# A first attention block written out in program order on VectorE and in the transfer queue, with more of the key sums on TensorE and one weight loaded later

## The chip, the cores and the metric

The kernel runs on one core of a Trainium2 chip. The metric is the time of one execution on the device in microseconds, as the median of repeated executions. Lower is better.

## What is computed

A single-head attention of 12288 queries over 768 pooled keys is followed by two feed-forward layers. The mean over 16 positions and the product with w_sr make keys that also serve as values.

```python
def _attn_ref(q, kv, w_sr):
    kv_pool = kv.reshape(B, H // r, r, W // r, r, C).mean(axis=(2, 4))      # r = 4: 768 keys, C = 128
    k = v = kv_pool.reshape(B, -1, C) @ w_sr
    s = (q @ k.transpose(0, 2, 1)) / np.sqrt(C)
    a = np.exp(s - s.max(-1, keepdims=True))
    a /= a.sum(-1, keepdims=True) + 1e-09
    return a @ v

def _moe_ref(x, w_in, w_out, alpha):        # 128 -> 2048 -> 128
    h = x @ w_in
    return (np.maximum(h, 0.0) + alpha * np.minimum(h, 0.0)) @ w_out

def _moe2_ref(x, w_in, w_out):              # 128 -> 2048 -> 128
    h = x @ w_in
    return (h * (1.0 / (1.0 + np.exp(-1.702 * h)))) @ w_out
```

## The kernel before

**Tiles and parts.** Everything is kept transposed: 128 channels on the partitions, tokens along the free axis. There are 24 blocks (NB) of 512 tokens. Each float32 operand of the large products is scaled by a power of two and split into two float16 halves, named with h and l (qh and ql, w1h and w1l), and each product is made of three float16 matmuls (`mm3`). The four weights w1 to w4 arrive as 64-bit words, two transfers of 1 MB each (`load_w`), and are turned into halves on the chip in three steps: `stats` finds the largest value (a reduction `wm` on VectorE for each MB, a row of small operations, a matmul of ones against `diag` that spreads the maximum over the partitions, and small operations that make scales), `conv1` and `conv2` assemble the numbers (one ScalarE pass, then three VectorE operations on 128x1024), and `conv3` splits them (a ScalarE cast for the high half, a GpSimd subtraction for the low one).

**The attention of a block j** has four tiles t of 128 queries. `a_q` and `q_split` scale and split the queries. `a_s` makes the scores of a tile (six matmuls into s) and takes the negated row maximum nm on VectorE. `a_e` takes the exponential on ScalarE with the row sum sm, and the reciprocal r on VectorE. `a_h` makes the high half ah on ScalarE and issues its transposing transfer into eh. `a_l` makes the low half al on VectorE and issues the transfer into el. `a_v` multiplies with the values into xacc. `x_scale` and `x_split` turn xacc into xh and xl, which the first layer reads.

**The layers** advance in steps t, sixteen steps (KF) for a block: `l1` with its ScalarE and VectorE activation at step t, `l2` four steps later, `l3` 31 and `l4` 36 steps later (`L2_LAG`, `L3_LAG`, `L4_LAG`). So TensorE has only two layers and the attention of a coming block to do until step 31.

**The time ahead of step 0.** The input transfers are issued first: q of block 0, w1, then kv in twelve transfers (`thirds`, four for each third of the keys), then w2, q of block 1 and w3. In the first third TensorE sums the 16 positions itself, by 16 matmuls that accumulate; in the other two VectorE reduces eight 128x1024 tiles, and one matmul for each third follows. `k_max` finds the largest key of each third, `v_scale` makes the scale and splits the keys into k_hi and k_lo, `x_bound` makes a bound from alpha that the scale of x needs. Block 0's attention then runs as part of the step loop, from step -18 on, by the tables `ATT_START`, `ATT_S` and `ATT_V`. The tables `STATS` and `PREP` place the other weights in the steps; w4 is loaded after step -8 (`W4_LOAD`).

**What sets the order.** A scheduler of the framework orders each engine's instructions when the program is built, by its own estimate; the order in the Python code is where it starts from. So the order in the built program isn't that of the code, and it is fixed: on the chip each engine runs its own list, and an instruction that waits holds up all that stand behind it. The transfers are all issued from the queue of SyncE, in a list of its own.

Of the kernel before, what the change touches and what calls it, by code (L numbers as in the profile page):

```python
# [39 lines left out]
ATT_START = [-18, -5] + [KF * j - 25 for j in range(2, NB)]  # L40
ATT_S = [(0, 2, 2, 6), (0, 3, 6, 9)] + [(0, 4, 7, 12)] * (NB - 2)
ATT_V = [(5, 8, 9, 12), tuple(range(12, 18))] + [(17, 18, 19, 21, 22, 22)] * (NB - 2)
# [11 lines left out]
def attn_moe_kernel(ctx: ExitStack, tc: tile.TileContext, q, kv, w_sr, w_in1, w_out1, alpha, w_in2, w_out2, out):  # L54
# [88 lines left out]

    def stats(*keys):

        n = len(keys)
        m = small("wm", F32, 2 * NCW)
        for i, key in enumerate(keys):
            for c in range(NCW):
                nc.vector.tensor_reduce(out=m[:, i * NCW + c:i * NCW + c + 1], in_=raw[key, c][:, :, 1].bitcast(F32),  # L150
                                        axis=AX.X, op=ALU.max, apply_absolute_value=True)
# [298 lines left out]
    def thirds(i):  # L450
        tk = slice(i * TK, (i + 1) * TK)
        for n in range(4):
# [3 lines left out]
            if i == 0:  # L456
# [5 lines left out]
        if i != 0:  # L462
# [12 lines left out]
    thirds(1)  # L475
    conv2(0)
    conv3(0)
    k_max(0)
    conv2(1)
    conv3(1)  # L480
    thirds(2)
# [57 lines left out]
    def step(t):  # L539
        pieces = [(j, t - ATT_START[j]) for j in range(NB) if -8 < t - ATT_START[j] < 26]  # L540
# [23 lines left out]
        for j, p in pieces:  # L564
# [6 lines left out]
            if p == -6 and j > 0:  # L571
                a_q(j)
            if p == -4 and j > 0:
# [4 lines left out]
        for f, lag in ((x_scale, -2), (x_split, -1), (y_scale, L2_LAG + KF), (y_split, L2_LAG + KF + 2)):  # L578
            if (x := at(t, lag)) and x[1] == 0:
                f(x[0])  # L580
        if x := at(t, L3_LAG):
# [4 lines left out]

    v_scale()
    q_scale(0)
    x_bound()
    for t in range(ATT_START[0], nstep + L4_LAG):  # L590
# [4 lines left out]
        if t == W4_LOAD:  # L595
            for c in range(NCW):
                load_w("w4", c)
        if t == KV_FREE:
            kv_ctx.close()
            g_p = ctx.enter_context(tc.tile_pool(name="gp", bufs=3, reuse_waits="tile"))  # L600
# [44 lines left out]
```

## Time and profile before

| | us |
|---|---|
| median of 3 runs | 1294.38 (1294.02 to 1294.47) |
| profiled execution, its own time | 1294.28 |
| span of its instructions | 1292.5 |
| TensorE busy | 1228.2 |
| ScalarE busy | 1107.2 |
| VectorE busy | 1036.0 |
| GpSimd busy | 780.6 |

The span is what lies between the first and the last instruction; 1.8 us of the execution's time lie around it. All times in the text are microseconds from the span's start. PE is TensorE, DVE is VectorE, ACT is ScalarE, POOL is GpSimd and SPq is the transfer queue of SyncE. Lines (L347) are those of the kernel before. A busy share is an average over stages with different limits, so the stages are looked at apart.

### The profile page before, as it was taken

To read this page: it belongs to the slowest core of one execution; us is meant where nothing else is said; L and a number is where in the kernel's file an instruction comes from. 1 tells how busy PE (TensorE), PEld (TensorE's weight loads), DVE (VectorE), ACT (ScalarE), POOL (GpSimd) and SP (SyncE) were. 2 spreads that over 40 slices of the span, in tenths; PEclk is the share of its full clock that TensorE was granted. 3 is DMA by queue.
4 is the path that set the end of the run, shared out by engine and by line. 5 is a ranking of instruction groups with operands and counts; after the bars stand their busy time and mean duration, and the time that the engine had idled before them with its cause. 6 is when DMAs were issued, how large, how long until landed. Compare 5 with 4: busy or idle time off the path is not lost.

```text
span 1292.5 us, 18032 instructions
## 1 busy us (share of the span) xinstructions
PE 1228.2 (95%) x5784; PEld 567.1 (44%) x5784; DVE 1036.0 (80%) x1879; ACT 1107.2 (86%) x1964; POOL 780.6 (60%) x670
## 2 busy tenths in 40 slices
PE   3468999999999999999999999999999999999998
PEld 2323444444444444444444444444444444444443
DVE  7988899778788787887887787787888878877666
ACT  1477899899898898898898998998988988988998
POOL 1046535576675676666665665756756666667774
PEclk8678999999999999999999999999999999999999
DMA  9713312122121221211221121221212212110000
GB/s 374 169 43 56 62 33 54 37 41 54 25 54 42 37 54 33 45 42 37 48 48 38 42 54 30 49 47 32 53 33 46 49 32 43 34 37 21 9 9 17
DMA packets 165375, 66.65 MB, mean 52 GB/s; under 512 B 156448, under 2 KB 156576, under 8 KB 164256
## 3 DMA queue, kind: packets, MB, share of 16 engines
q1 hardware_dynamic: 165280, 65.51, 21.9%
q8 instruction: 45, 0.74, 0.2%
q14 instruction: 50, 0.41, 0.1%
HBM read 21.05 MB, written 6.29 MB: 21 GB/s over the span
## 4 chain that ended last, share of the span: by engine, by line
PE 55%; ACT 16%; DVE 13%; issue 5%; DMA 0%; POOLq 0%; ACTq 0%
PE h L103 8%; PE h L105 7%; PE h L104 7%; PE y L104 7%; PE y L105 7%; PE y L103 7%; DVE g L347 4%; ACT g L346 4%; ACT g L401 3%; ACT s L255 3%; DVE g L402 2%; ACT g1h L354 2%; PE xacc L103 2%; PE xacc L104 2%; PE xacc L105 2%
## 5 line engine op out<-in xcount | busy, mean ns | idle before, releaser
L355 POOL TENSOR_TENSOR g1l<-g,g1h 128x512 f16<-128x512 f32 x384 | 457.0, 1196 | 324.9 <-ACT g1h L354 308.8
L411 POOL TENSOR_TENSOR g2l<-g,g2h 128x512 f16<-128x512 f32 x272 | 315.4, 1160 | 120.5 <-ACT g2h L409 110.9
L401 ACT ACTIVATE g<-h,yu 128x512 f32<-128x512 f32 x384 | 269.4, 702 | 103.9 <-PE h L105 100.8
L402 DVE SCALAR_TENSOR_TENSOR g<-g,h 128x512 f32<-128x512 f32 x384 | 262.5, 684 | 110.6 <-ACT g L401 104.9
L347 DVE SCALAR_TENSOR_TENSOR g<-g,oma,h 128x512 f32<-128x512 f32 x384 | 284.9, 742 | 53.1 <-ACT g L346 47.1
L354 ACT CAST g1h<-g 128x512 f16<-128x512 f32 x384 | 244.3, 637 | 7.2 <-PE y L105 5.6
L346 ACT ACTIVATE g<-h 128x512 f32<-128x512 f32 x384 | 236.2, 615 | 15.3 <-PE h L105 8.0
L409 ACT CAST g2h<-g 128x512 f16<-128x512 f32 x384 | 243.8, 635 | 3.3 <-PE y L105 1.2
L104 PE MATMUL y<-g1l,w2h 128*128 128x512 f16 x384 | 145.5, 379 | 8.7 <-POOL g1l L355 8.7
L103 PE MATMUL h<-xh,w1h 128*128 128x512 f16 x384 | 146.5, 383 | 5.2 <-ACT xh L320 4.1
L103 PE MATMUL h<-yh,w3h 128*128 128x512 f16 x384 | 145.2, 378 | 4.2 <-DVE g L347 1.1
L104 PE MATMUL h<-xl,w1h 128*128 128x512 f16 x384 | 146.6, 382 | 1.4
L105 PE MATMUL h<-xh,w1l 128*128 128x512 f16 x384 | 146.7, 382 | 0.0
L103 PE MATMUL y<-g1h,w2h 128*128 128x512 f16 x384 | 145.6, 379 | 1.2 <-ACT g1h L354 1.2
L104 PE MATMUL y<-g2l,w4h 128*128 128x512 f16 x384 | 145.5, 379 | 0.5 <-POOL g2l L411 0.5
L105 PE MATMUL y<-g2h,w4l 128*128 128x512 f16 x384 | 145.5, 379 | 0.0
L105 PE MATMUL y<-g1h,w2l 128*128 128x512 f16 x384 | 145.5, 379 | 0.0
L103 PE MATMUL y<-g2h,w4h 128*128 128x512 f16 x384 | 145.5, 379 | 0.0
L105 PE MATMUL h<-yh,w3l 128*128 128x512 f16 x384 | 145.4, 379 | 0.0
L104 PE MATMUL h<-yl,w3h 128*128 128x512 f16 x384 | 145.3, 378 | 0.0
L245 DVE TENSOR_REDUCE nm<-s 128x1 f32<-128x768 f32 x96 | 91.5, 953 | 14.2 <-PE s L240 10.6
L411 DVE TENSOR_TENSOR g2l<-g,g2h 128x512 f16<-128x512 f32 x112 | 90.0, 804 | 9.7 <-ACT g2h L409 9.7
(227 smaller groups left out, 1664.8 us busy)
## 6 DMA issues: line engine op xcount, KB each, us to landing
q<-in_q SPq DMA_DIRECT2D x24, 256.0 KB, 2.6
kv<-in_kv SPq DMA_DIRECT2D x12, 512.0 KB, 9.9
out<-ob SPq DMA_DIRECT2D x24, 256.0 KB, 2.0
raw_w<-in_moe_w_in SPq DMA_DIRECT2D x4, 1024.0 KB, 9.7
raw_w<-in_moe_w_out SPq DMA_DIRECT2D x4, 1024.0 KB, 6.9
eh<-ah SPq DMA_TRANSPOSE x96, 2.7
wsr<-in_w_sr SPq DMA_DIRECT2D x1, 64.0 KB, 2.7
al<-in_moe_alpha SPq DMA_DIRECT2D x1, 8.0 KB, 1.8
```

The lines of the kernel that those rows point to most:

```text
L103: mm(out=o, lhsT=wh, rhs=xh, start=start, stop=False)
L104: mm(out=o, lhsT=wh, rhs=xl, start=False, stop=False)
L105: mm(out=o, lhsT=wl, rhs=xh, start=False, stop=stop)
L245: nc.vector.tensor_reduce(out=nm, in_=s[:, :, 0:HALF], axis=AX.XY, op=ALU.max, negate=True)
L346: nc.scalar.activation(g, h, AF.Relu, scale=-1.0)
L347: nc.vector.scalar_tensor_tensor(out=g, in0=g, scalar=oma[:, m:m + 1], in1=h, op0=ALU.mult, op1=ALU.add)
L354: nc.scalar.copy(hi, g)
L355: nc.gpsimd.tensor_tensor(out=lo, in0=g, in1=hi, op=ALU.subtract)
L401: nc.scalar.activation(g, h, AF.Tanh, scale=ysc[j][:, 0:1])
L402: nc.vector.scalar_tensor_tensor(out=g, in0=g, scalar=1.0, in1=h, op0=ALU.add, op1=ALU.mult)
L409: nc.scalar.copy(hi, g)
L411: e.tensor_tensor(out=lo, in0=g, in1=hi, op=ALU.subtract)
```

## The change

Block 0's attention leaves the step loop. Its calls are written out in the code ahead of the loop, and from `v_scale` to the end of step 2 the framework's manual schedule keeps VectorE and the transfer queue in the order of the code. ScalarE, TensorE and GpSimd are still ordered by the scheduler. TensorE sums the second third of kv too (the host lays that third out like the first), so VectorE reduces four tiles, not eight. `x_bound` stays behind `v_scale`. The query split of block 1 stands inside block 0's attention. The reductions of w2's maximum stand between pieces of the attention, w2's conversion behind it, and w4 is loaded after block 0's last transposing transfer. The reductions for w3 and w4 come at step 1, as before in the code, but VectorE may no longer do them earlier.

```diff
-ATT_START = [-18, -5] + [KF * j - 25 for j in range(2, NB)]
-KV_FREE = -11
-W4_LOAD = -8
-STATS = {-9: ("w2",), 1: ("w3", "w4")}
-PREP = [(-8, -7, -6), (-7, -6, -5), (2, 3, 4), (5, 6, 7), (10, 11, 12), (13, 14, 15)]
+ATT_START = [None, -5] + [KF * j - 25 for j in range(2, NB)]
+MANUAL_END = 2
+X_SCALE = -2
+STATS = {1: ("w3", "w4")}
+PREP = [(2, 3, 4), (5, 6, 7), (10, 11, 12), (13, 14, 15)]
...
+    def w_max(key, c, keys):
+        if keys not in wm:
+            wm[keys] = sm_p.tile([P, 2 * NCW], F32, tag="wm", name="wm")
+        i = keys.index(key) * NCW + c
+        nc.vector.tensor_reduce(out=wm[keys][:, i:i + 1], in_=raw[key, c][:, :, 1].bitcast(F32), axis=AX.X, op=ALU.max,
+                                apply_absolute_value=True)
...
-        c, p = scale_of(qsc[j], ps_x.tile([P, TB], F32, tag="x", name="qt"), None, "q")
+        c, p = scale_of(qsc[j], bank("qt"), None, "q")
...
-            if i == 0:
+            if i < 2:
                 for r in range(4):
                     mm(out=pks[i], lhsT=wsr, rhs=t[:, r * TK:(r + 1) * TK], start=n + r == 0, stop=n + r == 6)
...
-    thirds(1)
     conv2(0)
     conv3(0)
-    k_max(0)
     conv2(1)
     conv3(1)
+    k_max(0)
+    thirds(1)
     thirds(2)
...
+    manual.enter_context(tc.manual_schedule(engines={nc.vector.engine, nc.sync.engine}))
     v_scale()
     q_scale(0)
     x_bound()
-    for t in range(ATT_START[0], nstep + L4_LAG):
+    a_s(0, 0); a_s(0, 1); flush()
+    a_q(1)
+    a_e(0, 0); a_e(0, 1); flush()
+    w_max("w2", 0, ("w2",))
+    a_h(0, 0); a_l(0, 0); a_s(0, 2); flush()
+    a_h(0, 1); a_l(0, 1); a_s(0, 3); flush()
+    q_split(1); flush()
+    a_e(0, 2); a_e(0, 3); flush()
+    a_v(0, 0); a_h(0, 2); a_l(0, 2)
+    a_v(0, 1); a_h(0, 3); a_l(0, 3); flush()
...
+    q_scale(1)
+    load_q(2)
+    for c in range(NCW):
+        load_w("w4", c)
+    w_max("w2", 1, ("w2",)); stats("w2")
+    conv1(2); conv1(3)
+    a_v(0, 2); a_v(0, 3); flush()
+    conv2(2); conv3(2)
+    x_scale(0); flush()
+    x_split(0); flush()
+    conv2(3); conv3(3)
+    for t in range(ATT_START[1] - 1, nstep + L4_LAG):
...
+        if t == MANUAL_END:
+            manual.close()
```

(Calls of one piece are put on one line here.)

The built programs differ in this way at the places that matter below. The first is VectorE's list where the scores of block 0 begin: nm is the row maximum, wm the reduction of a weight, and ov to kxc are the chain of `x_bound` that starts from a matmul (pm). Before:

```order
L150 TENSOR_REDUCE wm_460<-raw_w21_247 128x1
L245 TENSOR_REDUCE nm_300<-s_293 128x1
L245 TENSOR_REDUCE nm_321<-s_314 128x1
L109 TENSOR_SCALAR nm_300<-nm_300,qu_278 128x1
L109 TENSOR_SCALAR nm_321<-nm_321,qu_278 128x1
L153 TENSOR_REDUCE wa_463<-wm_460 128x1
L150 TENSOR_REDUCE wm_615<-raw_w30_251 128x1
```

And after:

```order
L125 TENSOR_REDUCE ov_299<-pm_297 128x1
L113 TENSOR_SCALAR ab_301<-ov_299,b_w1_160 128x1
L111 TENSOR_SCALAR ab_301<-ab_301 128x1
L113 TENSOR_SCALAR kx_105<-ab_301 128x1
L113 TENSOR_SCALAR kxc_107<-kx_105 128x1
L257 TENSOR_REDUCE nm_313<-s_306 128x1
L111 TENSOR_SCALAR nm_313<-nm_313,qu_291 128x1
L257 TENSOR_REDUCE nm_321<-s_314 128x1
L111 TENSOR_SCALAR nm_321<-nm_321,qu_291 128x1
```

The weights' reductions have left the place between the scores, and the chain of `x_bound`, which the scheduler had worked into the scaling of the keys, now stands ahead of the first row maximum. The second place is VectorE's list behind the first layer's first activations, after the change: g1 is that activation for a step, nm and al are of block 1, and raw_w30 to raw_w41 are the two MB each of w3 and w4.

```order
L292 SCALAR_TENSOR_TENSOR al__608<-e_583,r_586,ah_598 128x768
L316 TENSOR_REDUCE ta_620<-q2_455 128x1
L111 TENSOR_SCALAR qd_619<-ta_620 128x1
L359 SCALAR_TENSOR_TENSOR g1_623<-g1_623,oma_104,h1_604 128x512
L257 TENSOR_REDUCE nm_618<-s_611 128x1
L111 TENSOR_SCALAR nm_618<-nm_618,qu_453 128x1
L153 TENSOR_REDUCE wm_628<-raw_w30_262 128x1
L153 TENSOR_REDUCE wm_628<-raw_w31_264 128x1
L153 TENSOR_REDUCE wm_628<-raw_w40_457 128x1
L153 TENSOR_REDUCE wm_628<-raw_w41_459 128x1
L257 TENSOR_REDUCE nm_741<-s_734 128x1
L165 TENSOR_REDUCE wa_633<-wm_628 128x2
```

All four reductions stand together behind two activations; before, they stood at four places of block 0's attention and of w2's conversion, ahead of the first layer. The third place is TensorE's list between the first layer's steps: h1 is a step's product, pm the matmul of w3's and w4's statistics that the row wa above leads to, and s the scores. The weight loads between the matmuls are left out. Before, the first two steps and what follows:

```order
L103 MATMUL h1_581<-xh_572,w1h_111 128x512
...
L103 MATMUL h1_591<-xh_572,w1h_111 128x512
...
L162 MATMUL pm_624<-diag_625,ones_95 128x128
...
L162 MATMUL pm_624<-diag_628,ones_95 128x128
...
L309 MATMUL qt_448<-qd_396,ones_95 128x1
...
L104 MATMUL h1_581<-xl_573,w1h_111 128x512
```

After, steps 0 and 1 are followed by scores of block 1 and two steps of the second layer, then come:

```order
L252 MATMUL s_734<-k_hi_98,ql_379 128x384
...
L174 MATMUL pm_637<-diag_638,ones_95 128x128
...
L174 MATMUL pm_637<-diag_641,ones_95 128x128
...
L105 MATMUL h1_672<-xh_541,w1h_111 128x512
...
L106 MATMUL h1_672<-xl_542,w1h_111 128x512
```

The product of step 2 (h1_672) now stands behind the two matmuls of the statistics.

## Rows read from the trace of the kernel before

**Rows 1.** The page: busy us of each engine, share of the span, instructions.

```profile
PE 1228.2 (95%) x5784; PEld 567.1 (44%) x5784; DVE 1036.0 (80%) x1879; ACT 1107.2 (86%) x1964; POOL 780.6 (60%) x670
```

**Rows 2.** Busy time by stretch: length, then each engine with instructions, clock, DMA.

```profile
29.00:68.60 39.60, 17.18 (x102) 10.85 (x103) 35.07 (x81) 13.94 (x20) 4.72 (x3) 0.59 0.66 172
68.60:87.00 18.40, 15.28 (x57) 6.34 (x57) 15.79 (x44) 14.12 (x23) 6.08 (x5) 0.78 0.22 50
87.00:120.10 33.10, 25.14 (x98) 10.23 (x97) 30.66 (x46) 23.92 (x39) 23.32 (x15) 0.88 0.27 48
120.10:139.50 19.40, 16.16 (x75) 7.07 (x75) 16.36 (x33) 15.71 (x29) 11.70 (x11) 1.00 0.37 76
...
200.00:300.00 100.00, 99.56 (x476) 45.79 (x474) 81.19 (x149) 89.97 (x163) 63.67 (x55) 1.00 0.21 43
```

**Rows 3.** Timeline, sums of kv: start, duration, engine, line, operation, count.

```profile
12.33 8.71 PE L458 MATMUL kp<-kv,wsr 128*128 128x256 f32 x30
...
27.54 3.45 DVE L460 TENSOR_REDUCE kvt<-kv 128x64 f32<-128x1024 f32 x3
...
32.65 1.21 DVE L150 TENSOR_REDUCE wm<-raw_w 128x1 f32<-128x1024 f32 x1
33.77 0.15 DVE L494 TENSOR_REDUCE v<-vm 128x1 f32<-128x3 f32 x1
```

**Rows 4.** Busy time by stretch, instructions on the tile kv alone; clock third from last.

```profile
12.90:16.20 3.30, 3.30 (x9) 2.66 (x8) 0.00 (x0) 1.00 1.03 417
16.80:20.90 4.10, 4.10 (x20) 3.39 (x18) 2.33 (x2) 1.00 1.02 408
...
23.60:31.00 7.40, 0.00 (x0) 0.00 (x0) 6.08 (x6) 0.50 1.03 422
```

**Rows 5.** Timeline, block 0's attention and the way to the first layer.

```profile
39.90 0.96 DVE L245 TENSOR_REDUCE nm<-s 128x1 f32<-128x768 f32 x1 [0.66 <-PE s L240]
...
42.99 0.99 ACT L255 ACTIVATE e<-s,nm,qu 128x768 f32<-128x768 f32 x1 [5.87 <-DVE nm L109]
...
57.53 1.02 DVE L280 SCALAR_TENSOR_TENSOR al__425<-e,r,ah 128x768 f16<-128x768 f32 x1 [0.33 <-DMA el<-al__355]
...
67.91 0.69 ACT L320 ACTIVATE xh<-xacc,xc 128x512 f16<-128x512 f32 x1 [2.95 <-DVE xc L111]
...
68.64 1.01 PE L103 MATMUL h<-xh,w1h 128*128 128x512 f16 x2 [2.95 <-ACT xh L320]
```

**Rows 6.** DMA issues: size, median us from issue to landing (to 100 us).

```profile
raw_w<-in_moe_w_out SPq DMA_DIRECT2D x4, 1024.0 KB, 6.9
...
eh<-ah SPq DMA_TRANSPOSE x7, 2.7
```

**Rows 7.** Timeline, VectorE beside GpSimd.

```profile
58.36 2.17 POOL L200 TENSOR_TENSOR w2l<-g,w2h 128x1024 f16<-128x1024 f32 x1 [28.93 <-ACT w2h L199]
...
58.47 3.15 DVE L190 SCALAR_TENSOR_TENSOR g<-raw_w,g 128x1024 int32<-128x1024 int32 x1
...
78.86 1.16 POOL L355 TENSOR_TENSOR g1l<-g,g1h 128x512 f16<-128x512 f32 x1 [2.49 <-DVE r L262]
...
79.14 0.20 DVE L109 TENSOR_SCALAR kt<-kt,kx 128x1 f32<-128x1 f32 x1
```

**Rows 8.** Groups on VectorE, 29.0 to 68.6: count, busy us, mean ns.

```profile
L150 DVE TENSOR_REDUCE wm<-raw_w 128x1 f32<-128x1024 f32 x6 | 7.3, 1209 | 0.0
```

**Rows 9.** The same from 68.6 to 87.0.

```profile
L347 DVE SCALAR_TENSOR_TENSOR g<-g,oma,h 128x512 f32<-128x512 f32 x6 | 4.4, 734 | 0.2 <-ACT g L346 0.2
L245 DVE TENSOR_REDUCE nm<-s 128x1 f32<-128x768 f32 x3 | 2.9, 953 | 1.9 <-PE s L240 1.9
...
L321 DVE SCALAR_TENSOR_TENSOR ql<-q,qc,qh 128x512 f16<-128x512 f32 x2 | 1.5, 740 | 0.0
L192 DVE SCALAR_TENSOR_TENSOR g<-raw_w,g 128x1024 int32<-128x1024 int32 x1 | 1.2, 1210 | 0.0
L280 DVE SCALAR_TENSOR_TENSOR al__547<-e,r,ah 128x768 f16<-128x768 f32 x1 | 1.0, 1006 | 0.0
```

More of the change, by code (lines that the diff above doesn't have):

```diff
@@ L38 @@
 L2_LAG, L3_LAG, L4_LAG = 4, 31, 36
-ATT_START = [-18, -5] + [KF * j - 25 for j in range(2, NB)]
-ATT_S = [(0, 2, 2, 6), (0, 3, 6, 9)] + [(0, 4, 7, 12)] * (NB - 2)
-ATT_V = [(5, 8, 9, 12), tuple(range(12, 18))] + [(17, 18, 19, 21, 22, 22)] * (NB - 2)
-KV_FREE = -11
-W4_LOAD = -8
-STATS = {-9: ("w2",), 1: ("w3", "w4")}
-PREP = [(-8, -7, -6), (-7, -6, -5), (2, 3, 4), (5, 6, 7), (10, 11, 12), (13, 14, 15)]
+ATT_START = [None, -5] + [KF * j - 25 for j in range(2, NB)]
+ATT_S = [None, (0, 3, 6, 9)] + [(0, 4, 7, 12)] * (NB - 2)
+ATT_V = [range(TB // P), tuple(range(12, 18))] + [(17, 18, 19, 21, 22, 22)] * (NB - 2)
+MANUAL_END = 2
+X_SCALE = -2
+STATS = {1: ("w3", "w4")}
+PREP = [(2, 3, 4), (5, 6, 7), (10, 11, 12), (13, 14, 15)]
 CW = 1024
@@ L142, in load_w @@
         raw[key, c] = t
+    wm = {}
+    def w_max(key, c, keys):
[4 more added lines that the diff above has]
+                                apply_absolute_value=True)
     def stats(*keys):
         n = len(keys)
[L147 to L151, printed above, removed]
+        if keys not in wm:
+            for key in keys:
+                for c in range(NCW):
+                    w_max(key, c, keys)
+        m = wm.pop(keys)
         a = small("wa", F32, 2)
@@ L539, in step @@
     def step(t):
-        pieces = [(j, t - ATT_START[j]) for j in range(NB) if -8 < t - ATT_START[j] < 26]
+        pieces = [(j, t - ATT_START[j]) for j in range(1, NB) if -8 < t - ATT_START[j] < 26]
         if x := at(t, L2_LAG):
@@ L570, in step @@
                     a_v(j, k)
-            if p == -6 and j > 0:
+            if p == -6 and j > 1:
                 a_q(j)
-            if p == -4 and j > 0:
+            if p == -4 and j > 1:
                 q_split(j)
@@ L577, in step @@
                     load_q(j + 1)
-        for f, lag in ((x_scale, -2), (x_split, -1), (y_scale, L2_LAG + KF), (y_split, L2_LAG + KF + 2)):
+        for f, lag in ((y_scale, L2_LAG + KF), (y_split, L2_LAG + KF + 2)):
             if (x := at(t, lag)) and x[1] == 0:
                 f(x[0])
+        for j in range(NB):
+            if j and t == KF * j + X_SCALE:
+                x_scale(j)
+            if j and t == KF * j + X_SCALE + 1:
+                x_split(j)
         if x := at(t, L3_LAG):
@@ L589, in attn_moe_kernel @@
     x_bound()
-    for t in range(ATT_START[0], nstep + L4_LAG):
+    a_s(0, 0)
+    a_s(0, 1)
+    flush()
+    a_q(1)
+    a_e(0, 0)
+    a_e(0, 1)
+    flush()
+    w_max("w2", 0, ("w2",))
+    a_h(0, 0)
+    a_l(0, 0)
+    a_s(0, 2)
+    flush()
+    a_h(0, 1)
+    a_l(0, 1)
+    a_s(0, 3)
+    flush()
+    q_split(1)
+    flush()
+    a_e(0, 2)
+    a_e(0, 3)
+    flush()
+    a_v(0, 0)
+    a_h(0, 2)
+    a_l(0, 2)
+    a_v(0, 1)
+    a_h(0, 3)
+    a_l(0, 3)
+    flush()
+    kv_ctx.close()
+    g_p = ctx.enter_context(tc.tile_pool(name="gp", bufs=3, reuse_waits="tile"))
+    q_scale(1)
+    load_q(2)
+    for c in range(NCW):
+        load_w("w4", c)
+    w_max("w2", 1, ("w2",))
+    stats("w2")
+    conv1(2)
+    conv1(3)
+    a_v(0, 2)
+    a_v(0, 3)
+    flush()
+    conv2(2)
+    conv3(2)
+    x_scale(0)
+    flush()
+    x_split(0)
+    flush()
+    conv2(3)
+    conv3(3)
+    for t in range(ATT_START[1] - 1, nstep + L4_LAG):
         if t == 0:
@@ L594, in attn_moe_kernel @@
         step(t)
[L595 to L600, printed above, removed]
+        if t == MANUAL_END:
+            manual.close()
         if t in STATS:
```

7 lines of the change are left out of this document (4 added, 3 removed).

## The prediction

> **What bounds the kernel now.** I read the page first: TensorE is busy for 1228 of 1292 us, but VectorE for 80% [rows 1], and these are averages. The second view is the busy time by stretch. From 200 on TensorE is busy 99.6% of the time at a granted clock of 1.00 [rows 2]: there it sets the time, and the change touches nothing there. So the change is worth what it moves the moment from which TensorE is full, near 139.5. Ahead of that it isn't the bound: from 29.0 to 68.6 it works 17.2 of 39.6 us at 0.59 of the clock, from 87.0 to 120.1 25.1 of 33.1, while VectorE works 35.1 of 39.6, 15.8 of 18.4 and 30.7 of 33.1 us [rows 2]. VectorE, with the waits between engines, paces all that lies ahead of 139.5. The third view, the timeline, gives the stations: the largest key is known at 33.77 [rows 3], the first row maximum starts at 39.90, the last low half at 57.53, and the first layer begins at 68.64 [rows 5].
>
> So two questions decide: when does the first layer start, and how much of VectorE's work is still open then?
>
> **Sums of kv.** In the trace 30 records (two for each matmul) of the first third take 8.71 us, to 21.04 [rows 3]. They come at two paces: 9 in 3.3 us at first, 20 in 4.1 us from 16.8 on, about 0.21 each [rows 4]; I take 0.216. The second third adds 16 matmuls, 32 records, 6.9 us. They write the tile that the first third's maximum is read from, and wait for that read (a reduction over 256 columns, 0.4 after 0.96 for 768 [rows 5]): from 21.6 to 28.6. The last third's single matmul follows, 0.6, and its maximum, 0.4. The largest key comes at 29.7. VectorE loses four reductions of 1.15 (three take 3.45 [rows 3]) and w2's reduction, which stood ahead of the key's maximum [rows 3]; with its other work it ends its four at 28.1, so TensorE is late by 0.6. **Gain 4.1 at this station**, 33.77 against 29.7.
>
> **Block 0 in strict order.** In the trace the first row maximum starts 6.1 behind the largest key, 39.90 less 33.77 [rows 3, 5]. Now the chain of x_bound stands ahead of it on VectorE, and its matmul behind eight matmuls of scores on TensorE, 0.3 to 0.4 each by two of 512 columns in 1.01 [rows 5]. That and five small operations of 0.2 [rows 7] put the row maximum 7.3 behind the key, at 37.0. From there I added the instructions of the two lists, each behind what it waits for: the row maximum 0.96, an exponential 0.99 [rows 5], its sum and reciprocal 0.6, a high half 0.93, a low half 1.02. The query split of block 1 costs 1.5 of waiting, since its low half stands ahead of the second pair's reciprocals and needs a ScalarE pass queued behind two exponentials. The last low half starts at 51.0, against 57.53 [rows 5], **6.5 earlier**; 4.1 of this was there already, the rest comes from w3's and w4's reductions being gone.
>
> **From there to the first layer.** The last two transfers of low halves are issued at 52.5 and 53.7 and land 2.7 later [rows 6], the last at 56.5. w2's statistics need a matmul that stands behind one of these landings (55.2); its scale is ready at 56.4, two ScalarE passes over 1024 columns follow (1.2, after 0.99 for 768 [rows 5]), and VectorE's shift of the second ends at 59.6. Only then comes the maximum of xacc over 512 columns, 0.7, at 60.4, then w2's two operations of 1.2 [rows 9], 62.8, and the scale of x, 63.2. On ScalarE w2's cast, 1.0, stands ahead of xh: 63.9, and xh 0.7 [rows 5]. **The first layer begins at 64.6, against 68.64: 4.0 earlier.**
>
> **w4 behind the attention.** Its two transfers, of 6.9 each [rows 6], leave the transposing ones alone. They are issued near 55.5 and landed by 63, and their reductions come at 81 or later. This costs nothing, with 18 us of cover.
>
> **What is still open on VectorE.** Behind the first layer's start the list now holds w2's second half (two operations of 1.2, the first held up by 0.7 beside GpSimd), block 1's scores, which run as single file (row maximum, wait for the exponential, reciprocal, low half), and four reductions of 1.21 for w3 and w4, which in the trace were all done ahead of the first layer, with w2's two: six in all [rows 8]. By the same addition these end at 84.0, the last row maximum of block 1 at 86, and TensorE, where the matmuls of the statistics stand ahead of step 2 of the first layer, starts that step at 87.3. At 87.0 in the trace VectorE has finished six activations of the first layer [rows 9]; now it has finished two. The ledger at 87.0:
> - open now and done before: four activations of 0.734, 2.9; the first half of w3 (a shift of 0.7, two operations of 1.2), 3.1; the query split of block 2 (0.74 and three small ones), 1.2; the statistics of w3 and w4 from the matmul on with the bounds of y, some 18 small ones of 0.16 on average, 2.9. Sum 10.1.
> - done now and open before: nearly two row maxima, with two small operations 2.1 (three stand in the row, the third barely begun), and a low half, 1.0 [rows 9]. Sum 3.1.
>
> **VectorE is 7.0 behind at 87.0**, although the first layer began 4.0 sooner and it is spared four reductions of 1.15, 4.6: by this ledger the strict list makes it wait 11.6 us more than the scheduler's list did.
>
> **What is made up by 139.5.** In the trace VectorE idles 2.4 of 33.1 us and 3.0 of 19.4 us there [rows 2]. An engine that is behind idles less. At the lower share of the two, 7%, it would idle 3.8 of the 5.4, and make up 1.6. The bounds are nothing and all 5.4. Behind 120 the order is nearly that of before, and TensorE's work behind 139.5 is the same. **Sum: 7.0 less 1.6 is 5.4 later.** The profiled execution took 1294.28, so 1299.7; the median is 0.1 above that execution, which I leave aside. My addition of the prologue may be off by 1.5 either way, so this case spans +0.1 to +8.5, 1294.4 to 1302.8.
>
> **A rule weighed.** GpSimd's subtractions hold up VectorE: an operation of two inputs took 3.15 beside a subtraction of 2.17 and 1.21 alone [rows 7, 9], which is the 0.7 above. A small operation on one column took 0.20 in the middle of another subtraction [rows 7], so I charge block 1's first reciprocal nothing. The Trainium skill, "SBUF — State Buffer", Who interferes with whom, says that tensor_scalar too can enter a mode that locks the ports shared with GpSimd, where its operands allow. By that the reciprocal's first step would wait for w2's second subtraction, 0.95 more, and the sum would be 1300.6; the row on the column speaks against it.
>
> **Rivals.**
> - *The backlog is absorbed.* The mechanism is the same, but VectorE's idle time ahead of 139.5 was slack, and all 5.4 go: 7.0 less 5.4 is 1.6 later, 1295.9, within what can be told. For it: TensorE idles 11.2 us in these stretches [rows 2]. Against: VectorE works 93% from 87.0 to 120.1, and its gaps are waits on other engines.
> - *Faster: the first layer's lead is kept.* If VectorE isn't what paces the steps behind 68.6, the first layer's earlier start carries through, 4.0 less: 1290.3. It decides if step 2 doesn't wait for w3's reductions, or if the idle time of 68.6 to 139.5, 2.6 and 5.4, takes up all that was postponed. For it: ScalarE and TensorE have room there. Against: step 2 stands behind the statistics in the list.
> - *The clock falls in the second third.* The granted clock was 0.50 once TensorE had nothing to do from 21.0 on [rows 4]. Now it pauses only 0.6. If it still fell, 32 records at the pace of the first nine would take 6.8 more, all on the path: 1306.5.
> - *The strict order isn't what the chip sees*: the built lists show it, so I give this nothing.
>
> **Chances.** The forecast 0.62, absorbed 0.18, faster 0.12, the clock 0.05, and 0.03 for a prologue with worse waits than these. A difference of 0.2%, 2.6 us, is about what can be told from none. Of the forecast's own span the part below 1297 is small; I count it with the absorbed case: same 0.19, slower 0.69, faster 0.12. The range leaves out the faster case, the clock's and a little at each end: 1294.0 to 1303.0.
>
> **What would show it.** The largest key near 29.7 with TensorE's records of the second third at 0.216; the last low half near 51; the first layer's first matmul near 64.6; then two activations of the first layer by 87, not six, with the four reductions standing ahead of step 2; VectorE's idle time up to 87 larger by more than 10 us; and the first layer's steps of block 1, which begin near 120 before, near 125. If step 2 runs by 75, or block 1's first layer by 120, I am wrong about the backlog. If the first layer begins behind 68, I am wrong about the prologue.

## The result and the profile after

The changed kernel takes 1303.97 us in the median (1303.38 to 1304.47) beside 1294.2 for the kernel before, measured with it. The ratio is 1.0076, with a 95% interval of 1.0059 to 1.0094: it is slower by 9.8 us. The forecast said slower, by 5.4, and its range ended at 1303.0, so the median lies 1.0 above it. The profiled execution took 1303.51, 9.2 more than that of the kernel before, over a span of 1301.7. All lines below are those of the changed kernel.

The page's busy row, to be read beside [rows 1]:

```profile
PE 1233.9 (95%) x5814; PEld 573.1 (44%) x5814; DVE 1033.3 (79%) x1875; ACT 1108.4 (85%) x1964; POOL 784.0 (60%) x670
```

The busy time by stretch, beside [rows 2] (length, then PE, PEld, DVE, ACT and POOL with instructions, the granted clock, DMA share, GB/s):

```profile
14.20:29.00 14.80, 14.28 (x62) 12.06 (x61) 12.21 (x14) 4.41 (x5) 4.26 (x2) 1.00 1.03 417
29.00:68.60 39.60, 20.27 (x115) 12.76 (x114) 28.68 (x73) 14.91 (x22) 2.12 (x1) 0.66 0.61 178
68.60:87.00 18.40, 9.11 (x24) 3.29 (x24) 14.24 (x28) 7.76 (x12) 4.76 (x3) 0.63 0.22 43
87.00:120.10 33.10, 22.24 (x92) 9.19 (x92) 30.40 (x54) 22.55 (x35) 19.74 (x12) 0.90 0.19 40
120.10:139.50 19.40, 14.25 (x68) 6.25 (x67) 16.38 (x35) 15.67 (x28) 15.23 (x10) 1.00 0.21 41
200.00:300.00 100.00, 99.56 (x475) 45.76 (x473) 81.57 (x149) 89.99 (x164) 60.87 (x53) 1.00 0.20 43
```

VectorE did not get more work, it waits more: 10.9 us in 29.0 to 68.6 and 4.2 in the next stretch, against 4.5 and 2.6. TensorE works 6.2 us less from 68.6 to 87.0. From 200 on it is busy 99.56 of 100 us, as before.

The stations, from the timeline (start, duration, engine, line, operation), answer to [rows 3, 5]:

```profile
29.82 0.16 DVE L506 TENSOR_REDUCE v<-vm 128x1 f32<-128x3 f32 x1
37.10 0.95 DVE L257 TENSOR_REDUCE nm<-s 128x1 f32<-128x768 f32 x1
51.02 1.01 DVE L292 SCALAR_TENSOR_TENSOR al__444<-e,r,ah 128x768 f16<-128x768 f32 x1
64.84 1.01 PE L105 MATMUL h<-xh,w1h 128*128 128x512 f16 x2 [3.86 <-ACT xh L332]
87.04 0.38 PE L174 MATMUL pm<-diag,ones 128*128 128x128 bf16 x2 [2.49 <-DVE diag L111]
87.26 0.38 PE L105 MATMUL h<-xh,w1h 128*128 128x512 f16 x1
129.24 0.81 PE L105 MATMUL h<-xh,w1h 128*128 128x512 f16 x3
```

Up to 87 each lies within 0.3 us of its forecast. The last row is the first layer of block 1: near 120 before, forecast near 125, now 129.2. So the step that failed lies between 87 and 129.

VectorE's timeline from the first layer to its step 2 shows the list at work (rows of the second and third score tile of block 1, and the reductions):

```profile
73.41 0.95 DVE L257 TENSOR_REDUCE nm<-s 128x1 f32<-128x768 f32 x1
...
75.82 0.15 DVE L273 TENSOR_SCALAR r<-sm 128x1 f32<-128x1 f32 x1 [1.21 <-ACT e L267]
...
76.09 0.73 DVE L359 SCALAR_TENSOR_TENSOR g<-g,oma,h 128x512 f32<-128x512 f32 x1
77.22 1.02 DVE L292 SCALAR_TENSOR_TENSOR al__608<-e,r,ah 128x768 f16<-128x768 f32 x1 [0.41 <-ACT ah L281]
...
78.95 0.73 DVE L359 SCALAR_TENSOR_TENSOR g<-g,oma,h 128x512 f32<-128x512 f32 x1
79.60 0.95 DVE L257 TENSOR_REDUCE nm<-s 128x1 f32<-128x768 f32 x1
...
80.72 4.59 DVE L153 TENSOR_REDUCE wm<-raw_w 128x1 f32<-128x1024 f32 x4
85.22 0.95 DVE L257 TENSOR_REDUCE nm<-s 128x1 f32<-128x768 f32 x1
```

The activation of step 0 (the first g) stands behind two score tiles and starts at 76.1, though its matmuls began at 64.8. Two activations are done by 87, where the kernel before had six [rows 9].

Two windows carry the accounting. The first is from 87 to VectorE's split of x for block 1 (xl, at 120.39 before and 128.44 after); the second is from 12 to the split for block 2 (154.5 and 163.8). Kernel before, then changed kernel:

```profile
87.00:120.39 33.39, 25.43 (x99) 10.38 (x98) 30.95 (x46) 24.21 (x39) 23.61 (x15) 0.88 0.27 48
12.00:154.50 142.50, 98.95 (x436) 49.04 (x435) 124.46 (x247) 83.84 (x134) 57.48 (x39) 0.81 0.48 131
```

```profile
87.00:128.44 41.44, 27.37 (x113) 11.23 (x113) 38.51 (x68) 29.56 (x47) 27.94 (x16) 0.92 0.17 36
12.00:163.80 151.80, 104.96 (x467) 54.99 (x466) 122.56 (x247) 85.37 (x135) 60.03 (x39) 0.84 0.42 123
```

Behind 87 VectorE works 38.5 us where it worked 30.9, and idles 2.9 where it idled 2.4: the backlog is 7.6, and none of it was made up. From 12 to block 2's split it works 1.9 us less and idles 11.2 us more, 29.2 against 18.0; this 9.3 is the whole difference, since the span ends 1138.0 behind that split before and 1137.9 after. The table further down uses the same window for every run.

### The profile page after: what moved, and what is told of

It is laid out like the page before. It is cut to its first block, busy times and chain, and to the rows that moved or that the text cites. A ratio compares the mean times of both kernels' runs of the same rounds, so it can differ in the third digit from the quotient of the medians.

```text
span 1301.7 us, 18090 instructions
## 1 busy us (share of the span) xinstructions
PE 1233.9 (95%) x5814; PEld 573.1 (44%) x5814; DVE 1033.3 (79%) x1875; ACT 1108.4 (85%) x1964; POOL 784.0 (60%) x670
## 4 chain that ended last, share of the span: by engine, by line
PE 56%; ACT 16%; DVE 13%; issue 7%; POOL 2%; POOLq 0%; ACTq 0%
PE h L105 8%; PE h L107 8%; PE h L106 8%; PE y L106 7%; PE y L107 7%; PE y L105 7%; DVE g L359 4%; ACT g L358 3%; ACT g L413 3%; ACT s L267 3%; ACT g1h L366 2%; DVE g L414 2%; PE xacc L106 2%; PE xacc L107 2%; PE xacc L105 2%
```

## Experiments: is it the strict order, and where?

Times are compared with those of the kernel before that were measured beside them. A number with a sign, such as +3.6, is the ratio less one, times 1294.4; the changed kernel stands at +9.8 (7.6 to 12.2). A station (a moment in a trace) is that of one profiled execution, which may lie some us from its run's median: e3's took 1.7 less, e6's 1.4 more, e5's 2.6 more.

**No strict order at all:**

```diff
-    manual.enter_context(tc.manual_schedule(engines={nc.vector.engine, nc.sync.engine}))
```

> The changed kernel without its manual schedule: its code order, its sums of kv and its late load of w4 stay, but the scheduler orders VectorE and the transfer queue. Theory A: without the strict order the reductions for w3 and w4 stand at four places ahead of or around the first layer's first steps, and the 9 to 10 us of loss go; with the gain of the kv sums 1290 to 1293. Rival D (the written-out calls and w4's late load cost, not the strict order): it stays above 1299.

Measured 1293.17, ratio 0.9987 (0.9978 to 0.9996), 1.7 faster than before. The loss is gone, D falls. Yet the largest key at 30.07 and the last low half at 51.6, as early as in the changed kernel, give little at the end: 1.7.

**Strict only until the loop, and strict only in the loop:**

```diff
+    manual.close()
     for t in range(ATT_START[1] - 1, nstep + L4_LAG):
```

> The changed kernel, with the manual schedule ended ahead of the step loop: block 0's attention and w2's conversion stay in strict order, block 1's scores and the first layer's steps are the scheduler's, which puts reductions of w3 and row maxima of block 1 between the pieces of block 0's attention. Theory A3 (the loss is made in the loop's strict steps, where block 1's scores run as single file and hold up the activations): step 2 of the first layer by 75, first layer of block 1 near 119 to 121, 1292 to 1295. Rival F (the loss is made in the strict order of block 0's attention, whose list waits 10.8 us between the largest key and the first layer, against 3.6 before): first layer of block 1 at 124 or later, 1298 or more.

Measured 1294.58, ratio 1.0001 (0.9991 to 1.0010), +0.1. So F falls, and A3 holds for the time; its step 2 came at 79.4, not by 75, in a profiled execution that took 1297.15. The second half is e12: the manual schedule is entered where this one is closed.

> The changed kernel with the manual schedule over the loop's steps -6 to 2 alone; block 0's attention ahead of them is the scheduler's. It is the complement of the run whose strict order ended at the loop (1294.6, as the kernel before), and it stands beside the run without any strict order (1293.2). Theory N (the two strict parts add: 1.4 for the first, so 9.4 for the second): 1302 to 1304. Theory O (they multiply: the first part's holes could be filled only with the work that the second part pins behind the first layer, so that either part alone costs little): 1294 to 1298, and VectorE's idle time up to the split of x of block 2 falls from 29 us to under 24.

Measured 1298.90, ratio 1.0028 (1.0017 to 1.0039), +3.6. Against no strict order the first part costs 1.8, the second 5.3, both together 11.5. So neither N nor O is right: the parts cost 4.4 more together than their sum (each of the four times has an interval of 1 to 2 us either way), while VectorE's idle time with the loop alone stays at 27.8. My reading is that what the list pins behind the first layer is missing as filling in the attention ahead of it, and that this is part of the price, not all; no run tries it on its own.

## Experiments: which of the strict instructions?

**The four reductions moved into the attention** (e3):

```diff
     w_max("w2", 0, ("w2",))
+    w_max("w3", 0, ("w3", "w4"))
...
+    w_max("w3", 1, ("w3", "w4"))
     a_e(0, 2)
...
+    w_max("w4", 0, ("w3", "w4"))
     x_split(0)
...
     conv3(3)
+    w_max("w4", 1, ("w3", "w4"))
```

> The changed kernel, strict order kept, with the four reductions for w3 and w4 taken out of the place ahead of the statistics: w3's two stand between pieces of block 0's attention, w4's two around the split of x. Theory A1 (the four reductions, 4.8 us, ahead of the statistics' matmul, are the larger part of the lag at 87): step 2 of the first layer starts near 83 instead of 87.3, and the loss of 9.7 falls by about 4: 1299 to 1300.5. Rival A2 (the single file of block 1's scores, each row maximum, exponential, reciprocal and low half waiting for the other, is the larger part): step 2 moves by under 2 us, 1302 to 1304.

Measured 1302.26, ratio 1.0060 (1.0043 to 1.0077), +7.8; step 2 at 85.1, which is 2.2 earlier in an execution whose largest key came 0.9 earlier (28.96). The time is A2's: 2 us of 9.8 hang on the reductions, which is hardly clear of the noise, so they are the smaller part.

**The statistics three steps later** (e4):

```diff
-STATS = {1: ("w3", "w4")}
-PREP = [(2, 3, 4), (5, 6, 7), (10, 11, 12), (13, 14, 15)]
+STATS = {4: ("w3", "w4")}
+PREP = [(5, 6, 7), (8, 9, 10), (12, 13, 14), (15, 16, 17)]
```

> The changed kernel with the statistics of w3 and w4 (and their conversions) placed three steps later in the code, behind the end of the strict order; TensorE's product of step 2 then stands ahead of the matmuls of the statistics. Theory A (the wait of step 2 behind the statistics is what costs): steps 2 and 3 of the first layer start before 75, GpSimd's idle stretch from 82 to 95 goes, and the time is 1292 to 1296. Rival E (VectorE's amount of work up to 139 decides, wherever the statistics stand): the lag at the first layer of block 1 stays 7 or more, 1301 to 1304.

Measured 1300.11, ratio 1.0042 (1.0028 to 1.0057), +5.4. That is neither A's time nor E's. TensorE no longer waits for the statistics with step 2 (72.48), but step 3 comes only at 82.12. On TensorE it stands behind two score tiles of block 1, which wait for exponentials (1.54 ahead of 75.50, and 2.67 below), and the activation of step 0, in VectorE's list behind block 1's scores, ends only at 81.23:

```profile
72.48 0.63 PE L105 MATMUL h<-xh,w1h 128*128 128x512 f16 x1
80.25 0.48 PE L248 MATMUL s<-k_hi,qh 128*128 128x384 f16 x1 [2.67 <-ACT e L267]
80.50 0.73 DVE L359 SCALAR_TENSOR_TENSOR g<-g,oma,h 128x512 f32<-128x512 f32 x1
82.12 0.63 PE L105 MATMUL h<-xh,w1h 128*128 128x512 f16 x1
```

**Block 1's attention two steps later** (e9):

```diff
-ATT_START = [None, -5] + ...
-ATT_V = [range(TB // P), tuple(range(12, 18))] + ...
+ATT_START = [None, -3] + ...
+ATT_V = [range(TB // P), (12, 13, 14, 15, 16, 16)] + ...
-    for t in range(ATT_START[1] - 1, nstep + L4_LAG):
+    for t in range(-6, nstep + L4_LAG):
```

> The changed kernel, strict order and reductions as they are, with block 1's attention two steps later in the code, so that two activations of the first layer and only two row maxima of block 1, not three, stand ahead of the statistics' matmul in VectorE's list. Theory A2 (the single file of block 1's scores, 4.7 to 6.2 us from one row maximum to the next in the profile after, holds up the statistics and with them step 2): step 2 starts 5 to 6 earlier, near 82, and of the 5.6 us the 2.6 that VectorE only waits in them are gained: 1300 to 1302. Rival A1 (the four reductions are what counts): step 2 and the time stay within 1 us of the changed kernel, 1303 to 1305.

Measured 1304.52, ratio 1.0080 (1.0065 to 1.0095), +10.4: no gain, and step 2 came at 85.3, not near 82. I had misread the list: behind the reductions, from 77.9 on, a low half and the third row maximum (83.4) still stand ahead of the statistics. The activations start 3 and 1.6 us earlier (73.2, 77.3), and VectorE's idle time rises from 29.2 to 32.2. An earlier row was worth nothing here, since the list waited as much further down. None of these three edits gives back more than 4.4 of the 9.8: no single row of them carries the loss.

## Experiments: what sets the pace behind 87?

**Less work for VectorE, less for GpSimd.** In e6 the second operation of `conv2` is left out for w3 and w4, so their lowest bits are missing. In e7 the subtraction of `conv3` is left out for them, so their low halves are zero:

```diff
+        if key in ("w1", "w2"):
             nc.vector.scalar_tensor_tensor(out=g, in0=raw[key, c][:, :, 0], scalar=29, in1=g,
```

```diff
+        if key in ("w1", "w2"):
             nc.gpsimd.tensor_tensor(out=wl[key][:, cs], in0=g, in1=wh[key][:, cs], op=ALU.subtract)
```

> The changed kernel, with one VectorE operation of each MB of w3 and w4 left out (the one that adds the lowest bits; four in all, 6.5 us in the profile after, between 87 and 129). Theory G (VectorE alone sets the pace from 87 to 129): the first layer of block 1 starts 5 to 6.5 earlier than 129.2, and the time falls by about as much, to 1298 to 1299.5. Rival H (GpSimd sets it, which is busy nearly without a pause from 95 to 130): under 2 us earlier, 1302 to 1304.

> The changed kernel, with GpSimd's four subtractions for the low halves of w3 and w4 left out (2.13 us each, 8.5 in all; the low halves are set to zero at the start, where GpSimd has nothing to do). Rival H (GpSimd sets the pace from 95 to 130): the first layer of block 1 starts 5 to 8 earlier than 129.2, 1296 to 1299. Theory G (VectorE sets it): VectorE is only relieved of what those four subtractions stretch, at most 3 us, and of the 1.1 us by which GpSimd's last subtractions hold up step 16: 1300 to 1303.

Measured e6 1297.89, ratio 1.0024 (1.0015 to 1.0034), +3.1; e7 1299.57, ratio 1.0036 (1.0022 to 1.0049), +4.7. Taking 6.5 us from VectorE gives 6.7 back (each of the two times has an interval of 1 to 2 us either way): G. Step 16, the first of block 1, came at 125.55, 3.7 earlier, in an execution whose largest key was 1.7 later (31.50). Taking 8.5 us from GpSimd gives 5.1, a time between those of G and H, and step 16 comes 4.0 earlier (the last line is VectorE's window up to that split, beside 87.00:128.44 above):

```profile
125.26 0.75 DVE L334 SCALAR_TENSOR_TENSOR xl<-xacc,xc,xh 128x512 f16<-128x512 f32 x1
125.28 0.38 PE L105 MATMUL h<-xh,w1h 128*128 128x512 f16 x1
```

```profile
87.00:125.26 38.26, 27.70 (x115) 11.39 (x115) 35.76 (x68) 30.09 (x48) 19.98 (x13) 0.91 0.20 41
```

VectorE's split is 3.2 earlier, and step 16 no longer trails it by 0.8. From 87 to the split VectorE works 2.75 us less than in the changed kernel, with the same number of instructions, and idles 0.4 less. So up to there VectorE sets the pace, and GpSimd acts mainly through it: it lengthens VectorE's operations beside it. By block 2's split (159.13 against 163.81) another 1.5 is gained, and that is idle time of VectorE, not work (27.45 and 27.46). At the end the gain is 1.0 more than the 4.1 that G allowed, and well short of 8.5.

**The kv sums of the kernel before in the strict list** (e15: `if i < 2` back to `if i == 0`, with the host's layout and the place of `thirds(1)`):

> The changed kernel with the kv sums of the kernel before; behind the largest key every row of VectorE's list stands as in the changed kernel. It prices the sums in the strict list. Theory T (a list in fixed order moves as a whole, so the 4.1 us of the largest key are all worth their length): everything behind the key 3.5 to 4.5 later than in the changed kernel, 1307.5 to 1308.5. Theory S (as in the three pairs of the scheduler's lists, where the sums on TensorE cost 1.9 to 2.1): 1301.5 to 1302.5.

Measured 1309.32, ratio 1.0105 (1.0090 to 1.0120), +13.6, so 3.8 more than the changed kernel; the two medians lie 5.35 apart, and the kernel before was 1.6 higher beside e15. This is T: in a fixed list the forecast's 4.1 at the largest key arrives at the end. In its profiled execution the key came 5.5 later, and none of that was made up:

```profile
35.30 0.15 DVE L506 TENSOR_REDUCE v<-vm 128x1 f32<-128x3 f32 x1
70.43 1.01 PE L105 MATMUL h<-xh,w1h 128*128 128x512 f16 x2 [3.86 <-ACT xh L332]
134.10 0.74 DVE L333 SCALAR_TENSOR_TENSOR xl<-xacc,xc,xh 128x512 f16<-128x512 f32 x1
```

These stations are 5.5, 5.6 and 5.7 later than in the changed kernel, and block 2's split, at 170.76, is 6.9 later. Here all that stands behind the key is late by about the same, so this is a shift of the whole list and not a backlog of VectorE alone; but it tries what the forecast leaned on, that lateness shortens VectorE's idle time, and it doesn't.

## Experiments: the sums of kv in the scheduler's lists

e1 is the kernel before with `if i < 2` and its layout; e14 is the version without strict order with `if i == 0`.

> The kernel before, with TensorE summing two thirds of kv and nothing else of the change. Theory A (the strict order of VectorE is what costs, the sums of kv are a gain of their own): the largest key comes near 29.7 instead of 33.77, the scheduler keeps w3's and w4's reductions ahead of the first layer, step 2 of the first layer follows its first step by some 3 us as in the kernel before, and most of the 4.1 us stays: 1290 to 1291.5. Rival B (whatever happens ahead of 87 is evened out behind it, because VectorE or GpSimd is full from 87 on): 1293.5 to 1294.5, first layer of block 1 at 120 as before. Rival C (the sums of kv themselves cost, through the clock or the transfers): 1296 or more.

> The version without strict order (1293.2) with the kv sums of the kernel before (two thirds on VectorE). It prices the sums on their own in this order. Theory R (VectorE sets the pace up to block 2, so four reductions of 1.15 us are worth about their sum): 1296.5 to 1298.5. Theory S (the gain at the largest key is lost in the list's waits before the layers are full): 1292.5 to 1294.5.

Measured e1 1297.12, ratio 1.0013 (1.0004 to 1.0022), +1.7: the sums alone don't help. Its VectorE timeline shows why:

```profile
30.24 0.42 DVE L466 TENSOR_REDUCE vm<-kp 128x1 f32<-128x256 f32 x1 [3.89 <-PE kp L458]
30.58 1.21 DVE L460 TENSOR_REDUCE kvt<-kv 128x64 f32<-128x1024 f32 x1
32.58 0.42 DVE L466 TENSOR_REDUCE vm<-pk 128x1 f32<-128x256 f32 x1 [0.79 <-PE pk L463]
33.04 0.16 DVE L494 TENSOR_REDUCE v<-vm 128x1 f32<-128x3 f32 x1
```

The scheduler put the second third's maximum, which waits 3.9 us for TensorE, ahead of the last reduction. The key comes at 33.04, and the first row maximum at 40.6 instead of 39.9. e1's measured time is that of rival C, but not for its causes: from 14.2 to 29.0 TensorE's granted clock is 1.00 (0.80 before), and the transfers bring 417 GB/s, as before. So it is shown where the gain went, but not where the 1.7 come from: the first layer starts 0.7 earlier than before (67.92), block 1's split is 0.2 later (120.58) and block 2's 1.8 later (156.24).

e14 measured 1291.17, ratio 0.9969 (0.9957 to 0.9980), 4.0 faster than before: without the sums this order is 2.3 better than with them (e2). Neither R nor S expected a gain. With the sums the first row maximum is 3.7 earlier (37.6 against 41.3), and the first layer starts at the same time (67.5 and 67.3). Which wait took it I have not settled: the scheduler made another list, and many rows changed places at once.

## Experiments: w4 behind the first layer of block 1

```diff
-    for c in range(NCW):
-        load_w("w4", c)
     w_max("w2", 1, ("w2",))
...
         step(t)
+        if t == 8:
+            for c in range(NCW):
+                load_w("w4", c)
...
-STATS = {1: ("w3", "w4")}
+STATS = {1: ("w3",), 16: ("w4",)}
-PREP = [(2, 3, 4), (5, 6, 7), (10, 11, 12), (13, 14, 15)]
+PREP = [(2, 3, 4), (5, 6, 7), (17, 18, 19), (22, 23, 24)]
```

This was put on the version without strict order (e8), on that with the old kv sums (e16), on the kernel before (e10) and on the kernel before with the new sums (e13), both by way of their tables `W4_LOAD`, `STATS` and `PREP`, and on the changed kernel (e11).

> As the run without strict order, and w4 is loaded after step 8 and its statistics and conversion are done from step 16 on, a good way behind the statistics of w3, so that VectorE's 8.6 us and GpSimd's 4.3 us for w4 fall behind the first layer of block 1. Theory I (the stretch up to the first layer of block 1 is full on VectorE and GpSimd, the one behind it has 7 us of VectorE and 15 us of GpSimd idle): first layer of block 1 by 114, 1288 to 1291. Rival J (what is postponed is missing as much behind): 1292.5 to 1295, with the third layer's first step at 151 or later as without it.

> The new order of the code without manual schedule, w4 behind step 16, and the kv sums of the kernel before. In three pairs of scheduler's lists the sums on TensorE cost 1.9 to 2.1 us. Theory S (they cost as much here): 1286 to 1287, faster than any version so far. Theory P (late w4 and the sums belong together): 1290 or more.

> The kernel before, with only w4's load put after step 8 and its statistics and conversion behind step 16. Theory I (VectorE is full up to the first layer of block 1, whatever the sums of kv are): most of the gain of the version with w4 behind comes from this alone, 1289 to 1291.5. Rival K (without the sums of kv on TensorE and the scheduler's other order the work that is freed is lost in waits): 1292.5 to 1295.

> The kernel before with the sums of two thirds of kv on TensorE and w4 behind step 16, in the old order of the code. Alone the first measured 1297.1 and the second 1296.8, against 1294.3 to 1295 of the kernel before; the version with both and the new order of the code 1288.4. Theory P (the two belong together: VectorE's saved 4.6 us and the late w4 make room that is only filled when both are there): 1288 to 1291. Theory Q (it is the new order of the code, from which the scheduler makes a list with fewer waits): 1294 to 1298.

> The changed kernel with its strict order, and w4 loaded after step 8, its statistics and conversion behind step 16. Theory L (the waits of the strict list and VectorE's work for w4 add up, since VectorE has hardly an idle moment behind 87 to make up either): the changed kernel's 1304 less the 5 to 6 us that this placing of w4 was worth without strict order, 1297.5 to 1299.5. Rival M (with w4 out of the way VectorE has room to make up what the strict list lost): 1290 to 1294.

| run | median us | ratio (interval) | VectorE busy, idle from 12 to block 2's split | split |
|---|---|---|---|---|
| before | 1294.2 | | 124.5, 18.0 | 154.5 |
| changed | 1303.97 | 1.0076 (1.0059 to 1.0094) | 122.6, 29.2 | 163.8 |
| e1 before, new kv sums | 1297.12 | 1.0013 (1.0004 to 1.0022) | 120.2, 24.0 | 156.2 |
| e2 no strict order | 1293.17 | 0.9987 (0.9978 to 0.9996) | 122.9, 18.8 | 153.7 |
| e5 strict until the loop | 1294.58 | 1.0001 (0.9991 to 1.0010) | 123.8, 21.7 | 157.5 |
| e14 no strict order, old kv sums | 1291.17 | 0.9969 (0.9957 to 0.9980) | 124.4, 17.1 | 153.5 |
| e8 no strict order, w4 later | 1288.37 | 0.9948 (0.9934 to 0.9963) | 119.8, 17.7 | 149.5 |
| e16 as e14, w4 later | 1292.99 | 0.9978 (0.9968 to 0.9988) | 125.9, 15.7 | 153.6 |
| e10 before, w4 later | 1296.80 | 1.0021 (1.0011 to 1.0032) | 121.2, 20.5 | 153.7 |
| e13 as e10, new kv sums | 1298.67 | 1.0033 (1.0023 to 1.0044) | 117.2, 26.9 | 156.1 |
| e11 changed, w4 later | 1300.70 | 1.0053 (1.0038 to 1.0068) | 119.7, 27.5 | 159.2 |

(Busy, idle and split are of one profiled execution each; e5's took 2.6 more than its median, e10's 1.8 less. In e10, e13, e11 and e16 the span ends 1138.8 to 1140.1 behind the split, in e8 1137.4, in e14 1136.2, in the first five rows 1137.9 to 1138.1.)

e8 beats both kernels, by 6.7 us (4.8 to 8.5) against before, and block 1's split comes at 108.46 instead of 120.39: I. From 87 to 107 TensorE works 18.3 of 20 us, where it works 14.9 in the kernel before and 14.6 in e2:

```profile
87.00:107.00 20.00, 18.29 (x84) 8.15 (x83) 15.43 (x32) 15.76 (x29) 13.41 (x10) 0.95 0.25 46
```

But the placing is no gain by itself. It gives 5.0 from e2 to e8 and 2.9 in the strict list (e11, less than L's 5 to 6 and far from M), and costs 1.2 from e14 to e16, 2.7 on the kernel before (e10, K with more than it asked for) and 2.6 from e1 to e13 (beyond Q's range, and far from P's). In e16 theory P of that run holds. In e10 block 1's split comes at 114.64, 5.8 earlier than before, and block 2's only 0.7 earlier: most of what is postponed is missing behind. The sums of kv are worth 3.9 in e8 (by e16), and cost 1.7 in e1, 2.3 in e2 (by e14) and 1.6 in e13 (by e10). The 1.2, the 1.6 and the 2.9 are no larger than the noise of the two times that each is made of. So neither edit has a price of its own in the scheduler's lists. Few waits alone don't decide it either: e16 has the least idle time of all, 15.7. What makes e8's list so much better I have not settled.

## Why the prediction was right and wrong

- **Sums of kv: right.** 29.82 for 29.7, TensorE at a granted clock of 1.00 through 14.2 to 29.0, so the clock rival fell. (Its price of 6.8 goes by records 0.43 us apart; the nine in 3.3 us of [rows 4] would give 4.8.) The 4.1 was priced by e15 at 3.8 of the end.
- **Strict order in block 0, and to the first layer: right** (37.10, 51.02 and 64.84 for 37.0, 51.0 and 64.6).
- **w4 behind the attention costs nothing:** not tried alone. In the trace its two reductions follow w3's without a pause (80.72, four in 4.59 us).
- **The ledger at 87: right in size and cause.** 7.0 forecast, 7.6 measured as VectorE's work up to block 1's split. VectorE's extra waits up to 87, forecast as 11.6, are 10.0 by the windows from 14.2 to 87 (17.7 against 7.7). That the 7.0 is so near is partly luck, since two errors offset each other. What the ledger left out is that the open work takes longer than it would have. GpSimd's subtractions, which were spread over 73 to 121 before, stop for 13.9 us and then follow each other from 95 on with pauses of 0.9 to 1.6, and VectorE's operations beside them are stretched. Below are VectorE's groups from 87 to 129.2 (count, busy us, mean ns, idle before). Alone these operations take 1.21 us [rows 9], 0.68 for the shift (77.15 in the kernel before) and 1.0 for the low half [rows 9]; so 6.6 us are stretch, against 4.9 by the same groups in the kernel before. These 1.7 are more than the missing 0.6: the ledger's own items were about 1.1 too many.

```profile
L204 DVE SCALAR_TENSOR_TENSOR g<-raw_w,g 128x1024 int32<-128x1024 int32 x4 | 6.5, 1627 | 0.0
L111 DVE TENSOR_SCALAR g<-g 128x1024 int32<-128x1024 int32 x4 | 6.2, 1562 | 1.0 <-ACT g L195 1.0
L202 DVE SCALAR_TENSOR_TENSOR g<-raw_w,g 128x1024 int32<-128x1024 int32 x4 | 5.4, 1340 | 0.0
L292 DVE SCALAR_TENSOR_TENSOR al__731<-e,r,ah 128x768 f16<-128x768 f32 x1 | 1.9, 1910 | 0.0
```

GpSimd's timeline where its pause ends:

```profile
80.41 1.16 POOL L367 TENSOR_TENSOR g1l<-g,g1h 128x512 f16<-128x512 f32 x1 [1.16 <-ACT g1h L366]
95.45 3.35 POOL L367 TENSOR_TENSOR g1l<-g,g1h 128x512 f16<-128x512 f32 x2 [13.88 <-ACT g1h L366]
```

- **"What is made up by 139.5": the step that failed.** I wrote that an engine that is behind idles less, and took 1.6 off. VectorE idled 5.7 us in the two stretches, against 5.5 before (5.4 by the rounded terms of the sum). All its gaps from 87 to block 1's split are waits on ScalarE and TensorE, and lateness didn't shorten them. The later stretch, from block 1's split to block 2's, shows it best, the changed kernel against e15, which is 5.7 later at its start (the changed kernel first):

```profile
128.44:163.81 35.37, 31.73 (x150) 14.17 (x149) 27.46 (x57) 28.10 (x51) 20.94 (x18) 1.00 0.32 64
134.10:170.80 36.70, 33.34 (x151) 14.52 (x150) 27.50 (x58) 28.13 (x51) 20.93 (x18) 0.96 0.31 62
```

VectorE works the same, and idles 7.9 us in the changed kernel and 9.2 in e15: the later list idles more. Of its six waits there, five are as long in both (3.2 us for exponentials, 1.6 for ScalarE's part of activations, three of 1.1 and less), and one, for scores from TensorE, grows from 1.3 to 2.6. In e7 and e6, whose split of block 1 is earlier (125.26 and 126.06), the idle time up to block 2's split is 6.4 and 6.2. So nothing of a lag was made up, and some was added; why the wait for the scores grows I have not settled (TensorE's granted clock is 0.96 in e15's stretch, 1.00 in the changed kernel's). I had named the waits on other engines as the argument against the absorbed case, and then subtracted all the same. The bounds of what is made up, nothing and 5.4, had no end on the other side, and the backlog grew: 7.6 plus 0.5 more idle time is the 8.05 at block 1's split, and step 16 is 9.2 late (120.05 before), not 8.05, because GpSimd holds up the products ahead of it; without its subtractions for w3 and w4 (e7) the step no longer trails the split.

The timeline ahead of that step (129.24, above), and TensorE's waits for GpSimd's low halves from 87 to 130 (total, times, longest; 4.0 in 4 times in the kernel before up to 121):

```profile
127.37 0.69 ACT L332 ACTIVATE xh<-xacc,xc 128x512 f16<-128x512 f32 x1
127.69 0.38 PE L106 MATMUL y<-g1l,w2h 128*128 128x512 f16 x1 [1.29 <-POOL g1l L367]
128.81 0.38 PE L106 MATMUL y<-g1l,w2h 128*128 128x512 f16 x1 [0.31 <-POOL g1l L367]
```

```profile
PE y L106 <- POOL g1l L367: 11.2, 10, 1.8
```

Step 16's input xh was ready at 128.06. With 7.0 and nothing made up the sum would have been 1301.3; the 1.6 that I took off is the largest single error. The other 2.2 us are 0.6 of work, 0.5 of idle time and the 1.1 of GpSimd's queue, which had no term.

- **The rule weighed: the trace decided rightly.** Block 1's first reciprocal step took 0.15 at 71.07, under a subtraction that runs from 69.90 for 2.12. By the Trainium skill, "SBUF — State Buffer", Who interferes with whom, it might have waited; on one column it did not: the sum that it reads was ready at 71.04.

```profile
71.07 0.15 DVE L273 TENSOR_SCALAR r<-sm 128x1 f32<-128x1 f32 x1 [1.21 <-ACT e L267]
...
69.90 2.12 POOL L212 TENSOR_TENSOR w2l<-g,w2h 128x1024 f16<-128x1024 f32 x1 [3.50 <-ACT w2h L211]
```

- **The rivals.** The absorbed backlog fell with the idle time that stayed at 5.7, and the first layer's kept lead with step 2, which began at 87.26 behind the statistics.

## What to carry to other kernels

When one engine sets the pace over a stretch and its order is fixed, a lag or a lead at the start of the stretch can arrive at its end in full, however much that engine idles there, because its gaps are waits on others that are as late. Here 7.6 became 9.2, and e15's 5.5 became 6.9. So price the recovery at nothing unless a trace shows it, and ask instead what the lag makes collide. Count an order written by hand by the idle time that its list leaves on the pacing engine up to the first moment from which the profiles agree. An edit worth its own length in a fixed list (3.8 us here for 4.1) can be worth less than nothing when a scheduler makes a new list from it, so try it in both.

## What the hardware showed that I had not expected

A one-source operation on VectorE with two columns was held up beside GpSimd, where those with one column were not. Counted over the whole trace of the kernel before, the tensor_scalar operations on one column that started under a subtraction took at most 0.22 us (175 of them), and the 22 on 128x2 float32 took 0.81 in the mean, against 0.22 for the four that met none. In the timeline of the kernel before a 128x2 shift took 1.80 us under a subtraction, against 0.15 for the operation on the same tile ahead of it:

```profile
64.05 0.15 DVE L109 TENSOR_SCALAR wa<-wa 128x2 f32<-128x2 f32 x1
...
65.03 2.12 POOL L200 TENSOR_TENSOR w2l<-g,w2h 128x1024 f16<-128x1024 f32 x1 [4.50 <-ACT w2h L199]
...
65.37 1.80 DVE L109 TENSOR_SCALAR wa<-wa 128x2 int32<-128x2 int32 x1
```

The Trainium skill, "VectorE: DVE Perf Modes", Mode 2×_2P — use both read ports for one tensor, says that such an operation may read the two halves of its source through two ports at once. These rows agree with it, since one column has no halves. GpSimd suffers too: its subtraction of 128x512 takes 1.16 us alone [rows 7] and 2.13 at 123.41 in the changed kernel.

Also, the largest key itself came at moments some us apart in kernels whose rows up to there are the same: 28.96 in e3, 29.82 in the changed kernel, 31.50 in e6. The time of these profiled executions goes with it (1.7 less than the median in e3, 1.4 more in e6), so distances from the key are safer to compare than stations. What moves the key I have not looked into.
